# State products on 64-row halves of the array, attention on quarter-column tiles, first-pass stores on SyncE's queue

## The chip, the core and the metric

The kernel runs on one core of a Trainium2 chip. TensorE (PE) multiplies matrices into PSUM, VectorE (DVE), ScalarE (ACT) and GpSimd (POOL) work on tiles, SyncE (SP) issues most transfers; ACT and POOL issue some. Each engine and each queue works through its instructions in order. The metric is the device time of one execution in microseconds; lower is better.

## What is computed

Cross attention between a sequence and a small set of state vectors, then two gated feed-forward networks, all from float64-typed data on the host:

```python
scores = scale * x @ state.T            # B,H,S,Ns = 8,8,512,32; D = 64
a = softmax(scores);   xread = a @ state
a2 = softmax(scale * state @ x.T);  sread = a2 @ x
h = concatenate([xread, sread], axis=2)         # rows S + Ns, H*D = 512 wide
h = ((h @ w1) * (h @ w2)) @ w3 @ w_out          # first network, 4608 rows
out = (sigmoid(h @ w_gate) * (h @ w_val)) @ w_out2
```

## The kernel before

Most products are made of three passes over numbers split in two float32r parts (`split`: ACT writes the high part, DVE or POOL the rest), a few over plain float32.

**State products.** `xread` is never formed for the sequence rows. Since `xread @ w1 = a @ (state @ w1)`, the kernel first multiplies each head's state by that head's 64 rows of w1 and w2 and stores the result `sw` in DRAM (`sw_d`); a batch then needs `aT` (the softmaxed scores) times its own `sw`. The states lie in `bd` as block-diagonal 128x128 tiles: 128 contraction rows are two heads of 64, 128 columns are four blocks of 32 states, and the blocks that belong to the other head are zero. A step (`sw_step`, line 337) takes one 128x512 block of w1 or w2, which `sw_prep` has loaded as raw 64-bit words (`raw`), converted (`m`, `r`: two ACT operations, then three of DVE, the last on line 101) and split (`wh`: ACT, then POOL). It makes two products for two pairs of batches, three passes each, so six matmuls of 128 rows; ACT copies both to `swst`, and ACT's queue stores them. Sixteen steps are a pass. The first pass (`bp0` = 0) comes at the start, for half the batches; the second (`bp0` = 2) is spread over the batches at places 1 and 2 of the order, eight steps in each, between the groups `pab` and `py` of the first network.

**A batch.** `ffn1` runs over eight column blocks j: `sw_weights` loads a block of `sw` (`swf`, two transfers of 64 partitions) two blocks ahead and splits it (`swh`); twelve matmuls (`pab`) and the gate (`asb`, `u`) follow; then four groups of 24 matmuls (`py`) with the product of w3 and w_out. Between them stands the attention, by slots: the state's reads of this batch (`a2t`, `sread` line 240, `sreadt` line 258) and the transposes and `scores` (line 177) of the next. The order on TensorE is the order of the code; on the other engines and on SP's queue the Tile scheduler sets it in this part of the program.

**Scores and reads.** `scores` makes four float32 matmuls, each with 128 contraction rows (two heads, against the block-diagonal `bd`), 64 columns, and one half of the PSUM partitions. A float32 matmul runs as two passes, so the trace shows eight. `sread` makes sixteen of 128 rows and 64 columns over 128 moving columns; half of each result (the other head) is not used. `sreadt` transposes twice and copies twice.

The rest, from about 620 us, is the second network with its own planner; the change doesn't touch it.

## Time and profile before

| | us |
|---|---|
| median of 3 runs (1411.93 to 1413.6) | 1411.97 |
| the profiled execution | 1415.93 |
| its span, first to last instruction | 1414.2 |
| TensorE busy | 1343.5 |
| VectorE busy | 924.7 |
| ScalarE busy | 750.2 |
| GpSimd busy | 278.3 |

The page gives shares over the whole span; the stages have different limits, so the stretches are read one by one. The first pass ends at about 72 us, batch 0 at 195, batches 1 and 2 at 257.5 and 321.5; the last of the eight ends at about 589, and the first network's remaining rows at 620. Waits are put down to what came last before the waiting instruction.

### The profile page before, as it was taken

The numbers are of one execution on the slowest core, as the hardware profiler recorded it, in microseconds if no ns is written. First come the engines' busy times: TensorE is split into PE (matmuls) and PEld (weight loads), VectorE is DVE, ScalarE is ACT, GpSimd is POOL, SyncE is SP. The second block draws the span as 40 slices with busy tenths as digits, with TensorE's granted clock in tenths as the row PEclk, the third lists the DMA queues.
The fourth block names the chain that finished last, engine by engine and source line by source line (L and its number), as shares of the span: only waits on it lengthen the run. The fifth ranks groups of instructions, "written<-read, shape, count | busy, mean of one in ns | idle before, by whom it ended". The sixth has DMA issues, their size and how long they took to land.

```text
span 1414.2 us, 18988 instructions
## 1 busy us (share of the span) xinstructions
PE 1343.5 (95%) x6560; PEld 1145.6 (81%) x6560; DVE 924.7 (65%) x1523; ACT 750.2 (53%) x1480; POOL 278.3 (20%) x255
## 2 busy tenths in 40 slices
PE   5669999999998999999999999999999999999997
PEld 3348877777876777898988998988988888988996
DVE  6789756645555566528677667778777677556543
ACT  6877656756445456436546546545545544433421
POOL 2352113324334234001121121021121110000000
PEclk9889999999999999999999999999999999999999
DMA  9867637754446354383343347655445694134132
GB/s 264 290 195 212 199 135 230 228 195 127 138 119 164 90 155 152 118 319 116 133 151 100 117 165 285 239 183 169 136 167 184 227 324 159 62 108 137 49 104 67
DMA packets 169128, 237.18 MB, mean 168 GB/s; under 512 B 46920, under 2 KB 111944, under 8 KB 166984
## 3 DMA queue, kind: packets, MB, share of 16 engines
q1 hardware_dynamic: 130536, 163.15, 36.6%
q10 hardware_dynamic: 37344, 63.39, 12.8%
q0 software_dynamic: 1152, 9.44, 1.9%
q8 instruction: 51, 0.84, 0.2%
q14 instruction: 45, 0.37, 0.1%
HBM read 150.99 MB, written 84.93 MB: 167 GB/s over the span
## 4 chain that ended last, share of the span: by engine, by line
PE 80%; DVE 6%; issue 5%; DMA 4%; POOL 2%; ACT 2%; ACTq 0%; SPq 0%; DVEq 0%; POOLq 0%
PE po L1019 19%; PE psA L922 18%; PE psB L922 9%; PE pab L112 8%; PE py L112 7%; PE psC L922 5%; PE pab L115 4%; PE py L115 4%; DMA yf<-yd 2%; PE pwp L112 2%; POOL wh L66 2%; PE pwp L115 1%; PE psr L245 1%; PE pxt L170 1%; DMA raw<-in_moe_w 1%
## 5 line engine op out<-in xcount | busy, mean ns | idle before, releaser
L922 PE MATMUL psA<-y,wt 128*128 128x448 f32 (+1 forms) x1440 | 304.6, 360 | 5.6 <-ACT u L61 2.8
L922 PEld LDWEIGHTS psA<-y,wt 128*128 128x128 f32 x1440 | 266.3, 188 | 25.8 <-ACT u L61 3.9
L1019 PE MATMUL po<-wo,p 128*128 128x512 f32 x1224 | 280.7, 389 | 0.4 <-DVE p L590 0.4
L1019 PEld LDWEIGHTS po<-wo,p 128*128 128x128 f32 x1224 | 229.5, 188 | 48.3 <-DVE p L590 1.0
L922 PE MATMUL psB<-y,wt 128*128 128x448 f32 (+1 forms) x720 | 161.1, 359 | 0.0
L66 POOL TENSOR_TENSOR o<-m,o 128x256 fp32r<-128x256 f32 x72 | 59.3, 823 | 503.3 <-ACT o L61 449.1
L112 PE MATMUL pab<-aT,swh 128*128 128x512 f32 x512 | 145.7, 407 | 12.2 <-ACT asb L61 4.7
L922 PEld LDWEIGHTS psB<-y,wt 128*128 128x128 f32 x720 | 133.5, 188 | 8.5
L112 PE MATMUL py<-u,wp 128*128 128x512 f32 (+1 forms) x576 | 132.2, 381 | 2.1 <-DVE u L66 1.7
L61 ACT ACTIVATE u<-psA 128x448 f32<-128x448 f32 (+1 forms) x120 | 63.9, 532 | 127.7 <-PE psA L922 103.0
L112 PEld LDWEIGHTS py<-u,wp 128*128 128x128 f32 x576 | 104.0, 189 | 28.5 <-issue 5.7
L66 POOL TENSOR_TENSOR swh<-swf,swh 128x512 fp32r<-128x512 f32 x64 | 90.8, 1424 | 167.9 <-ACT swh L61 155.0
L112 PEld LDWEIGHTS pab<-aT,swh 128*128 128x128 f32 x512 | 95.3, 193 | 35.0 <-ACT asb L61 6.4
L61 ACT ACTIVATE p<-sg 128x448 fp32r<-128x448 f32 (+1 forms) x120 | 67.9, 566 | 86.6 <-DVE sg L958 79.0
L434 DVE TENSOR_TENSOR asb<-asb,pab 128x512 f32<-128x512 f32 (+1 forms) x72 | 47.0, 654 | 98.8 <-PE pab L115 90.3
L101 DVE CUSTOM_DVE_ANT_0 m<-m,r 128x1024 uint16<-128x1024 uint16 (+1 forms) x116 | 80.1, 692 | 11.1 <-ACT r L90 1.3
L66 DVE TENSOR_TENSOR u<-asb,u 128x512 fp32r<-128x512 f32 (+1 forms) x72 | 65.9, 916 | 30.7 <-ACT u L61 30.1
L1034 DVE TENSOR_TENSOR ob<-po,ob 128x512 f32<-128x512 f32 x68 | 46.8, 688 | 58.7 <-PE po L1019 55.4
L115 PE MATMUL pab<-aT,swh 128*128 128x512 f32 x256 | 81.7, 401 | 2.0 <-POOL swh L66 2.0
L922 PE MATMUL psC<-y,wt 128*128 128x448 f32 (+1 forms) x360 | 80.9, 360 | 1.1 <-DVE s L955 1.1
L61 ACT ACTIVATE y<-yf 128x448 fp32r<-128x448 f32 (+1 forms) x120 | 63.1, 558 | 32.4 <-DMA yf<-yd 32.4
L98 DVE SCALAR_TENSOR_TENSOR m<-raw,m 128x512 uint32<-128x512 uint32 (+1 forms) x116 | 78.2, 676 | 3.2
(118 smaller groups left out, 2028.3 us busy)
## 6 DMA issues: line engine op xcount, KB each, us to landing
raw<-in_moe_w SPq DMA_DIRECT2D x48, 512.0 KB, 5.6
wt<-wd SPq DMA_DIRECT2D x12, 1792.0 KB, 7.6
part<-ob SPq DMA_DIRECT2D x68, 256.0 KB, 2.8
ob<-part SPq DMA_DIRECT2D x68, 256.0 KB, 3.9
yf<-yd SPq DMA_DIRECT2D x37, 448.0 KB, 4.0
swd<-swst ACTq DMA_DIRECT2D x32, 512.0 KB, 4.1
swf<-swd SPq DMA_DIRECT2D x128, 128.0 KB, 3.7
wd<-o ACTq DMA_DIRECT2D x56, 256.0 KB, 2.3
```

Source lines behind the costliest of these rows:

```text
L61: return nc.scalar.activation(out=o, in_=i, func=AF.Copy)
L66: (sub or nc.vector).tensor_tensor(out=lo, in0=src, in1=hi.bitcast(F32), op=ALU.subtract)
L98: nc.vector.scalar_tensor_tensor(out=mu, in0=hi, scalar=0x80000000, in1=mu, op0=ALU.bitwise_and, op1=ALU.bitwise_or)
L101: nc.vector.tensor_tensor(out=m.bitcast(I32), in0=m.bitcast(I32), in1=r, op=ALU.add)
L112: nc.tensor.matmul(o, w[i], xx[k], start=n == 0 and i + k == 0, stop=False)
L115: nc.tensor.matmul(o, w[1 - late], xx[late], start=False, stop=n == len(pairs) - 1)
L170: nc.tensor.transpose(pt[:, c * P : (c + 1) * P], xn[b][:, g, c].rearrange("p a d -> p (a d)"), ident)
L245: nc.tensor.matmul(pt[64 * q : 64 * q + 64, k], t["a2"][:, k, c, 64 * q : 64 * q + 64], xn[b][:, 2 * k + q, c].rearrange("p a d -> p (a d) ...
L434: p2["dve"] = nc.vector.tensor_tensor(out=asb[:, :n], in0=asb[:, :n], in1=pab[1][:, :n], op=ALU.mult)
L922: nc.tensor.matmul(o, w[:, i, kb * P : (kb + 1) * P], xx[kb][h], start=start, stop=i == 1 and kb == 1, skip_group_check=True,)
L1019: nc.tensor.matmul(o, pt[j][i][:, s * P : (s + 1) * P], wot[j][:, h], start=j == js[0] and i + h == 0, stop=j == js[-1] and i == 1,)
L1034: nc.vector.tensor_tensor(out=ob, in0=o, in1=ob, op=ALU.add)
```

## The change

The states lie transposed but not block-diagonal, in `stT`: 64 rows are one head, the upper half of the partitions holds the even heads and the lower half the odd ones. A step still has six matmuls of 128 columns by 512, each with 64 contraction rows: the two heads' products go to two PSUM banks from the two halves of the array's rows. A step covers four consecutive batches, so the batches run in the order 0 to 7. `scores` has eight matmuls of 64 rows by 32 columns, `sread` 32 of 128 rows by 32 columns over 64 moving columns; `sreadt` has one transpose and one copy. Only half the states are turned at the start, the other half after the fifth step, and `z` is not cleared; six of its eight loads go out on ACT's queue. `swf` is one transfer of 128 partitions. In the first pass the stores of `swst` leave by SP's queue, in the second by ACT's.

```diff
-    sw_d = dram.tile([2, 2, 2, 2, P, B // 2, 512], F32, name="swd")
+    sw_d = dram.tile([2, 2, G, NS, 4, 2, 2, 512], F32, name="swd")
...
-                for k in range(2):
-                    pt = ps_at.tile([P, 512], F32, tag="at", name="psc")
-                    for q in range(2):
+                pts = [ps_at.tile([P, 512], F32, tag="at", name="psc") for _ in range(2)]
+                for g in range(G):
+                    for k in range(2):
                         nc.tensor.matmul(
-                            pt[64 * q : 64 * q + 64],
-                            bd[:, 2 * k + q, bp, b2 * 64 : b2 * 64 + 64],
-                            t["xT"][:, 2 * k + q],
+                            pts[k][NS * g : NS * g + NS],
+                            stT[64 * k : 64 * k + 64, g, b * NS : (b + 1) * NS],
+                            t["xT"][64 * k : 64 * k + 64, g],
...
-                        for q in range(2):
+                        for g in range(G):
                             nc.tensor.matmul(
-                                pt[64 * q : 64 * q + 64, k],
-                                t["a2"][:, k, c, 64 * q : 64 * q + 64],
-                                xn[b][:, 2 * k + q, c].rearrange("p a d -> p (a d)"),
+                                pt[NS * g : NS * g + NS, k],
+                                t["a2"][:, k, c, NS * g : NS * g + NS],
+                                xn[b][:, g, c, k],
...
-                for k in range(2):
-                    nc.tensor.transpose(
-                        pt[:, k].rearrange("p q h n -> p (q h n)"), t["sr"][:, k], ident
-                    )
+                nc.tensor.transpose(
+                    pt.rearrange("p g n -> p (g n)"), t["sr"].rearrange("p k d -> p (k d)"), ident
+                )
...
+        for b in range(B):
+            (nc.sync if b in (1, 3) else nc.scalar).dma_start(
...
-            products(*[(po[q], [([t[:, g, q] for t in bds], wh)]) for q in range(2)], late=1)
-            for q in range(2):
-                copy("act", st[:, q], po[q])
-            nc.scalar.dma_start(out=sw_d[hf, g % 2, g // 2, a, :, bp0 : bp0 + 2], in_=st)
+            for m, (x, w) in enumerate(((0, 0), (1, 0), (0, 1))):
+                for k in range(2):
+                    nc.tensor.matmul(
+                        po[k],
+                        sts[x][64 * k : 64 * k + 64, g],
+                        wh[w][64 * k : 64 * k + 64],
+                        start=m == 0,
+                        stop=m == 2,
+                    )
+            for k in range(2):
+                copy("act", st[:, k], po[k])
+            (nc.scalar if h4 else nc.sync).dma_start(
...
-        order = [q * (B // 2) + bp for bp in range(B // 2) for q in range(2)]
+        order = list(range(B))
...
-                for q in range(2):
-                    nc.sync.dma_start(
+                nc.sync.dma_start(
```

What moves in the order is shown at three places. TensorE in batch 1, at `sread` and the step behind it (`psr` are the reads, `psw` the products, `wh` the two parts of the weight block, `bds` or `sts` those of the states). Before:

```order
L115 MATMUL pab<-aT_1665,swh_1737 128x512 x2
L245 MATMUL psr<-xn,a2tr 64x128 x16
L112 MATMUL psw<-wh_1819,bds_1487 128x512
L112 MATMUL psw<-wh_1819,bds_1488 128x512
L112 MATMUL psw<-wh_1819,bds_1487 128x512
L112 MATMUL psw<-wh_1819,bds_1488 128x512
L115 MATMUL psw<-wh_1820,bds_1487 128x512 x2
L112 MATMUL pab<-aT_1665,swh_1770 128x512
```

Now:

```order
L115 MATMUL pab<-aT_1667,swh_1738 128x512 x2
L246 MATMUL psr<-xn,a2tr 32x64 x32
L344 MATMUL psw<-wh_1819,sts_1490 128x512 x2
L344 MATMUL psw<-wh_1819,sts_1491 128x512 x2
L344 MATMUL psw<-wh_1820,sts_1490 128x512 x2
L112 MATMUL pab<-aT_1667,swh_1770 128x512
```

The places are the same; the reads are twice as many and smaller, and the two matmuls of a row of the step now go to the two halves of the rows.

SP's queue from the start to the first loads of batch 0's `swf`. Before:

```order
L80 DMA raw<-in_moe_w 128x1024 x2
L290 DMA z<-in_state 32x16x64 x4
L80 DMA raw<-in_moe_w 128x1024
L155 DMA xn<-in_x 128x4x64 x8
L80 DMA raw<-in_moe_w 128x1024 x13
L465 DMA swf<-swd 64x4x128 x4
L80 DMA raw<-in_moe_w_out 128x1024
```

Now, from the eleventh weight block on:

```order
L80 DMA raw<-in_moe_w 128x1024 x2
L353 DMA swd<-swst 128x1024
L80 DMA raw<-in_moe_w 128x1024 x2
L353 DMA swd<-swst 128x1024 x2
L80 DMA raw<-in_moe_w 128x1024 x2
L353 DMA swd<-swst 128x1024 x5
L80 DMA raw<-in_moe_w_out 128x1024
L353 DMA swd<-swst 128x1024
L80 DMA raw<-in_moe_w_out 128x1024
L353 DMA swd<-swst 128x1024 x3
L475 DMA swf<-swd 128x4x128 x3
L80 DMA raw<-in_moe_w_out 128x1024 x2
```

The sixteen stores stand between the loads, and the first `swf` stands behind the last of them.

ScalarE in the second half of the first pass (`swst` are the copies of the products). Before:

```order
L61 ACTIVATE wh_423<-m 128x512
L345 DMA swd<-swst 128x1024
L89 ACTIVATE m<-raw 128x512
L90 ACTIVATE r<-raw 128x512
L61 ACTIVATE swst<-psw 128x512 x2
L89 ACTIVATE m<-raw 128x512
L61 ACTIVATE wh_448<-m 128x512
L345 DMA swd<-swst 128x1024
L90 ACTIVATE r<-raw 128x512
```

Now:

```order
L61 ACTIVATE wh_418<-m 128x512
L90 ACTIVATE r<-raw 128x512
L61 ACTIVATE swst<-psw 128x512 x2
L61 ACTIVATE wh_443<-m 128x512
L61 ACTIVATE swst<-psw 128x512 x2
L61 ACTIVATE wh_468<-m 128x512
L61 ACTIVATE swst<-psw 128x512 x2
L61 ACTIVATE wh_493<-m 128x512
L89 ACTIVATE m<-raw 128x512
L61 ACTIVATE swst<-psw 128x512 x2
```

`m` and `r` now run several steps ahead of the `wh` that rest on them, and the stores are gone from this queue.

## Rows read from the trace of the kernel before

**Rows 1.** The page's first part: busy us, share, instructions.
```profile
PE 1343.5 (95%) x6560; PEld 1145.6 (81%) x6560; DVE 924.7 (65%) x1523; ACT 750.2 (53%) x1480; POOL 278.3 (20%) x255
```

**Rows 2.** Stretches: length, busy by engine, granted clock, DMA share, GB/s.
```profile
core 0: us, PE busy (x) PEld busy (x) DVE busy (x) ACT busy (x) POOL busy (x), PEclk, DMA share, GB/s
5.50:35.60 30.10, 19.18 (x75) 12.86 (x75) 22.59 (x38) 22.71 (x44) 9.18 (x6) 0.89 0.97 280
35.60:72.30 36.70, 23.75 (x62) 13.31 (x62) 24.81 (x32) 29.84 (x55) 13.59 (x10) 0.81 0.83 282
75.00:115.00 40.00, 30.86 (x132) 22.55 (x132) 36.61 (x44) 28.52 (x53) 23.57 (x16) 0.83 0.73 196
...
195.00:257.50 62.50, 61.77 (x307) 49.60 (x306) 38.76 (x53) 42.95 (x78) 22.18 (x16) 1.00 0.61 188
...
321.50:545.00 223.50, 215.38 (x1082) 172.56 (x1081) 126.49 (x174) 120.11 (x215) 81.19 (x69) 0.98 0.44 130
...
620.00:1414.00 794.00, 777.81 (x3751) 695.45 (x3749) 534.07 (x959) 378.94 (x801) 90.70 (x104) 1.00 0.46 158
```

**Rows 3.** Timeline of TensorE in batch 1: start, length, instructions merged.
```profile
229.60 1.07 PE L112 MATMUL psw<-wh,bds 128*128 128x512 f32 x4
...
231.05 1.94 PE L186 MATMUL psc<-xT,bd 128*64 128x512 f32 x8
232.92 3.96 PE L112 MATMUL py<-u,wp 128*128 128x512 f32 x16
...
238.53 1.07 PE L112 MATMUL psw<-wh,bds 128*128 128x512 f32 x4
...
239.89 3.79 PE L112 MATMUL py<-u,wp 128*128 128x512 f32 x16
...
245.33 1.07 PE L112 MATMUL psw<-wh,bds 128*128 128x512 f32 x4
```

**Rows 4.** The same timeline, at the reads of the state.
```profile
207.73 1.07 PE L112 MATMUL pab<-aT,swh 128*128 128x512 f32 x4
...
209.18 1.97 PE L245 MATMUL psr<-xn,a2tr 128*64 128x128 f32 x32
211.08 1.19 PE L112 MATMUL psw<-wh,bds 128*128 128x512 f32 x4
...
212.58 1.07 PE L112 MATMUL pab<-aT,swh 128*128 128x512 f32 x4
```

**Rows 5.** Passes of `psc` and `psr`: ns, shortest, median, longest.
```profile
L186 PE MATMUL psc<-xT,bd x64: 592/592/643, 19.6 to 512.5; 128*64 128x512 f32 x64
...
L245 PE MATMUL psr<-xn,a2tr x256: 272/273/476, 107.4 to 548.6; 128*64 128x128 f32 x128
```

**Rows 6.** Timeline of TensorE: the transposes of `sreadt` in batch 1.
```profile
219.38 0.39 PE L261 MATMUL psrt<-ident,sr 128*128 128x128 f32 x2
```

**Rows 7.** ScalarE's waits from 35.6 to 72.3 us: total, times, longest.
```profile
ACT wh L61 <- DVE m L101: 5.6, 9, 0.7
```

**Rows 8.** SP's queue, first pass: start, length, transfers merged.
```profile
13.49 33.81 SPq L80 DMA_DIRECT2D raw<-in_moe_w  x13
51.00 3.80 SPq L465 DMA_DIRECT2D swf<-swd  x4
54.91 0.54 SPq L80 DMA_DIRECT2D raw<-in_moe_w_out  x1
```

**Rows 9.** Transfers from 0 to 75 us: count, KB, median us to landing.
```profile
raw<-in_moe_w_out SPq DMA_DIRECT2D x4, 512.0 KB, 5.1
...
swf<-swd SPq DMA_DIRECT2D x6, 128.0 KB, 6.2
```

**Rows 10.** Timeline of TensorE at the end of the first pass.
```profile
70.64 0.73 PE L115 MATMUL psw<-wh,bds 128*128 128x512 f32 x2 [0.18 <-POOL wh L66]
75.03 1.72 PE L112 MATMUL pab<-aT,swh 128*128 128x512 f32 x4 [3.66 <-ACT swh L61]
```

**Rows 11.** Timeline of TensorE in batch 5.
```profile
450.95 1.09 PE L170 MATMUL pxt<-ident,xn 128*128 128x128 f32 x4 [5.89 <-issue]
```

More of the change, by code (lines that the diff above doesn't have):

```diff
@@ L284, in tile_state_attention__then__gated_ffns, with state_turn @@
         tc.swap_default_side()
-        z = p1.tile([P, B // 2, G, 2, D], F32, name="z", bufs=1)
-        nc.vector.memset(z, 0.0)
-        for b2 in range(2):
-            for h2 in range(2):
-                p0 = b2 * 64 + h2 * 32
-                nc.sync.dma_start(
-                    out=z[p0 : p0 + NS, :, :, h2, :].rearrange("p b g d -> p (b g) d"),
-                    in_=state[b2 * (B // 2) : (b2 + 1) * (B // 2), h2::2].rearrange(
-                        "b g n d -> n (b g) d"
-                    ),
-                )
-        for g in range(G):
-            pt = ps_main.tile([P, 512], F32, tag="m", name="pt")
-            for bp in range(B // 2):
-                nc.tensor.transpose(
-                    pt[:, bp * P : (bp + 1) * P], z[:, bp, g].rearrange("p a d -> p (a d)"), ident
-                )
-            copy("act", bd[:, g].rearrange("p a b -> p (a b)"), pt)
-        def state_split(pool, bp0):
-            t = [pool.tile([P, G, 2, P], F32R, name=f"bds{i}", bufs=1) for i in range(2)]
-            for g in range(G):
-                split(t[0][:, g], t[1][:, g], bd[:, g, bp0 : bp0 + 2])
-            return t
+        z = p1.tile([P, 2, H, D], F32, name="z", bufs=1)
+        for b in range(B):
+            (nc.sync if b in (1, 3) else nc.scalar).dma_start(
+                out=z[b % 4 * NS : b % 4 * NS + NS, b // 4],
+                in_=state[b].rearrange("h n d -> n h d"),
+            )
+        def state_turn(h4):
+            pt = ps_main.tile([P, 512], F32, tag="m", name="pt")
+            for g in range(G):
+                nc.tensor.transpose(
+                    pt[:, g * P : (g + 1) * P],
+                    z[:, h4, 2 * g : 2 * g + 2].rearrange("p a d -> p (a d)"),
+                    ident,
+                )
+            copy("act", stT[:, :, h4 * P : (h4 + 1) * P], pt.rearrange("p (g m) -> p g m", g=G))
+        state_turn(0)
         def ahead(prep, depth, count):
@@ L354, in tile_state_attention__then__gated_ffns @@
         for i in range(2 * JF):
-            sw_step(i, 0, bds, wh(i), p1)
+            sw_step(i, 0, sts, wh(i), p1)
             if i == 0:
@@ L475, in prep @@
                 split(t[0], t[1], f, sub=nc.gpsimd)
-                return [[t[i][:, :, a] for i in range(2)] for a in range(2)]
+                return [[t[i][:, a] for i in range(2)] for a in range(2)]
             return ahead(prep, 2, JF)
```

61 lines of the change are left out of this document (34 added, 27 removed).

## The prediction

> **What bounds the kernel now.** I read the page's busy shares first: TensorE is busy nearly the whole span [rows 1], so the average says nothing about where a change can pay; the table by stage does [rows 2]. Four stretches matter. In the first pass of the state products (to about 72 us; the row is its second half) no engine is full: ScalarE is busy 29.84 of 36.70 us, VectorE 24.81, TensorE 23.75 at a mean granted clock of 0.81. In the start of batch 0 (75 to 115) VectorE is the bound, 36.61 of 40. From 115 us on TensorE is: 61.77 of 62.50 us in batch 1 (195 to 257.5), in which half of the second pass lies, and 215.38 of 223.50 in batches 3 to 6. The two gated-FFN passes after 620 us are TensorE's too, and the change touches nothing there. So TensorE time saved between 115 and 589 us counts in full as long as the others have room (in batch 1 ACT is busy 42.95 of 62.50 us, DVE 38.76), and in the first pass it counts for nothing: there the question is what the queues and ScalarE do.
>
> Then the timeline of TensorE inside batch 1 [rows 3, 4], which has the three kinds of matmul that change, each beside plain ones. A plain 128x512 one has a pitch of 0.227 us: six of `psw` from 238.53 to 239.89 are 1.36. The scores `psc` and the products `psr` already run on two 64-column halves of the array, and the rows show what that is worth: each pass of `psc` takes 592 ns and eight of them take 1.94 [rows 3, 5], so they run in four rounds of two, (1.94 - 0.59) / 3 = 0.45 us apart with the entry in it, 0.43 without. `psr`: 32 passes of 273 ns in 1.97 us, 16 rounds of two at 0.11. Two halves thus run at the same time without loss. And entering and leaving the halves costs: six `psw` last 1.45 before `psc` against 1.36, and the 24 `py` after it 5.61 (232.92 to 238.53) against 5.44 (239.89 to 245.33); with the 1.87 between, the excursion costs 0.09 + 1.87 + 0.17 = 2.13, of which 4 x 0.43 = 1.72 streams and **0.41 is the change of tiling**. For `psr` it is 0.09 + 1.90 + 0.14 = 2.13, with 1.74 of streaming and 0.39 of change. I use 0.40.
>
> **State products, second pass.** In batches 1 and 2 sixteen `sw_step`s of six matmuls stand between the `pab` and `py` groups, 1.36 us each. The change keeps six, but each has 64 contraction rows; the upper and the lower half of the array work for different heads and banks. Three rounds of two are 3 x 0.227 = 0.68, plus 0.40 for leaving and re-entering full tiling, since the neighbours stay full: 1.08, a gain of 0.28 x 16 = 4.5 us. No row has a matmul under 128 contraction rows. Bounds from the rows: halves overlap as the column halves do and the tiling change costs nothing where a step stands beside `psr` or `psc`, about -6; halves run one after the other, 1.36 + 0.40, +6.4. I take the overlap, because the column halves are the nearest row, and they overlap within one round. The Trainium skill (TensorEngine Tiling (Array Packing), Theoretical Speedup) gives up to 2x for a contraction of 64 or less, which would be that same 0.68; no run here shows it for rows.
>
> **Scores.** The four matmuls of 64 columns become eight of 64 rows by 32 columns, two passes each. If all eight tiles run together it is 2 rounds x 0.43 + 0.41 = 1.27 against 2.13: -0.86 in each of the seven batches whose scores lie in TensorE's stretch, **-6.0 us**. The first batch's lie in the first pass and count 0. The other bound is that only two column tiles stream at once, as now: 0.
>
> **Reads of the state (`sread`).** 16 matmuls of 64x128 become 32 of 32x64, so 64 passes instead of 32. With four tiles at once and half the columns it is 16 rounds x 0.055 + 0.40 = 1.27 against 2.13, -0.86 x 8 = -6.9. But per pass that is 14 ns, and the fastest pace in any row is 1.74 / 32 = 54 ns [rows 4]. If no faster pace is to be had, 64 x 0.054 + 0.40 = 3.86, +1.7 a batch, +14 in all. No row decides; the queue of instructions is filled during the plain matmuls before, which speaks for a burst. I take half the gain, **-3.5**.
>
> **`sreadt`.** One transpose instead of two, and one copy instead of two. Two of 270 ns take 0.39 [rows 6], so one less is 0.12 x 8 = **-0.9**. The copy is VectorE's and hidden.
>
> **First pass.** The order shows what moves. ScalarE loses the sixteen store issues; they cost it little (0.33 us on its queue, beside a running copy). More important, it now runs `m` and `r` of several steps ahead of `wh`, where before each `wh` waited for VectorE's last operation on the `r` issued just before: nine such waits are 5.6 us [rows 7], and ScalarE's whole idle time there is 36.70 - 29.84 = 6.9 [rows 2]. I count 7 us of it as removable at best. TensorE's half of the pass is hidden under ScalarE, so its halved matmuls bring nothing, as does the missing clear of `z` at the start, where the transfers are the limit. Against it stands SyncE. Its queue is in order, and each store waits there for ScalarE's copies; behind it are the loads of `raw`, and behind all sixteen the first loads of batch 0's `swf`. Before, `raw` went out in one run from 13.49 to 47.3 and the first `swf` at 51.00, over twenty us before use, with w_out from 54.91 on [rows 8]. The `raw` loads keep four and more steps of lead in the new order, so I cost that at nothing; what covers them is six buffers, and if the lead is gone each late one is a landing of about 5 us [rows 9]. But `swf` is now issued after the last copy: about 1.1 (copies) + 0.3 (store) + 0.6 (issue) + 6.2 (landing, rows 9) + 0.6 (`swh`) = 8.8 us after the last product, where the gap now is 75.03 - 71.37 = 3.66 [rows 10]: +5.1. Between them: **-2**, with ends -7 (idle gone, and VectorE fills the gap with w_out) and +5 (nothing gained, the gap longer).
>
> **Not in the sum.** At 445 us TensorE waits 5.89 us for a transpose [rows 11]: the copy that frees its bank stands on VectorE behind work that waits, over ScalarE, for a late `swf`. The order there is the same after the change, only with one `swf` transfer instead of two. If it goes, the time falls by up to 5.9; I leave it.
>
> **Sum.** -4.5 - 6.0 - 3.5 - 0.9 - 2 = -16.9. The profiled execution took 1415.93 us (its span 1414.2): 1399.0. It lay 3.96 above the median 1411.97, so against the median the forecast is **1395.1 us**.
>
> **Rivals.**
> (a) *The quarters give no more than the halves.* Scores and `sread` stay as they are, the rest holds: -4.5 - 0.9 - 2 = -7.4, 1404.6. For: no row has more than two column tiles streaming. Against: the two that do lose nothing.
> (b) *Slower: changes of tiling that aren't repaid.* If upper and lower rows take turns, each `sw_step` costs 0.40 more, +6.4; the scores, whose two row halves then take turns too, stay at four rounds (0), and `sread` gives nothing. With -0.9 and -2 it is +3.5: 1415.5. It decides at 0.40 of the 0.68 us: a step pays only if more than that overlaps. For: sixteen new excursions, each certain. Against: the overlap of the column halves.
> (c) *The pace of instructions.* 64 passes at 54 ns, +14 instead of -3.5: +0.6 in all, 1412.6. The Trainium skill (TensorE: Matmul & The Clock Gate, Back-to-back issue gap) names some 62 ns per matmul when the sequencer decodes in software; by it `sread` would take 64 x 0.062 + 0.40 = 4.4 us and the sum would be about +4.5, an estimate from that page; the 54 ns of this trace are already under it.
> (d) *SyncE's queue.* The first pass ends +5 and the late `swf` costs VectorE's stretch another 3: -6.9 in all, 1405.1. For: VectorE is nearly full from 75 to 115. Against: it has w_out to convert meanwhile.
>
> **How the numbers follow.** Forecast 0.58, (a) 0.14, (b) 0.10, (c) 0.08, (d) 0.10. A measurement tells about 0.2% (2.8 us) from no change. Forecast, (a) and (d) are faster, 0.82; (c) is within, 0.08; (b) slower, 0.10. The forecast's own range goes from -28 (first pass -7, products -6, `sread` -6.9, part of the wait at 445 us) to -8, and reaches over (a) and (d); leaving out (b), (c) and the far low end is about 0.2: 1384 to 1410.
>
> **What would show it.** In the profile after: `psw` matmuls starting in pairs, a step in batches 1 and 2 at 1.0 to 1.1 us from the `pab` before to the `pab` behind (1.7 for (b)); the sixteen passes of the scores in about 1.1 us from the first start to the last end (1.9 for (a)); `psr` under 1.5 us of 64 passes (3.5 for (c)); TensorE's stretch from batch 1 to batch 7 shorter by about 14; the first `pab` between 70 and 76 us, after a gap of 6 to 9 us behind the last `psw`. I am wrong if that stretch is not shorter, or if the first pass ends later than 80 us.

## Result and profile after

The changed kernel takes **1387.34 us** in the median (1385.52 to 1390.18), the kernel before 1411.95 beside it: a ratio of 0.9828, 95% interval 0.9807 to 0.9849, 24.6 us less. The forecast was 1395.1 with a range of 1384 to 1410. The profiled execution took 1387.57 us (span 1385.7), 28.4 less than the profiled one of before, which lay above its median.

First the page's busy line and the table of stretches, to be held against [rows 1, 2]; its columns are length, busy time by engine, granted clock of TensorE (1.00 is 2.4 GHz, 0.50 is 1.2), DMA share and GB/s.

```profile
PE 1310.1 (95%) x6864; PEld 1113.3 (80%) x6864; DVE 911.1 (66%) x1514; ACT 744.8 (54%) x1478; POOL 283.1 (20%) x255
...
35.60:72.30 36.70, 20.13 (x72) 10.46 (x72) 24.81 (x38) 29.20 (x55) 19.24 (x12) 0.55 0.75 268
75.00:115.00 40.00, 27.10 (x164) 20.06 (x164) 33.24 (x41) 28.08 (x51) 22.85 (x16) 0.87 0.79 225
195.09:253.53 58.44, 57.68 (x345) 43.09 (x346) 37.14 (x52) 41.63 (x78) 22.90 (x16) 1.00 0.62 199
312.66:511.11 198.45, 196.42 (x1189) 158.11 (x1188) 119.28 (x162) 110.94 (x200) 75.62 (x62) 1.00 0.45 142
```

The first line of the table is the second half of the first pass: ScalarE is about as busy as before (29.20 us against 29.84), VectorE is the same to the digit, GpSimd has gone up from 13.59 to 19.24, and TensorE's granted clock has fallen from 0.81 to 0.55. In the second line VectorE has 33.24 us of the 40 where it had 36.61. The two batch stretches are TensorE's, nearly without a gap, as before.

Where the time went is read from the start of each batch's first `pab` (first network) in the two timelines, us:

| stage | before | after | difference |
|---|---|---|---|
| start to the end of the first pass | 71.37 | 71.46 | +0.1 |
| gap before the first `pab` | 3.66 | 7.30 | +3.6 |
| batch 0 | 119.85 | 116.33 | -3.5 |
| batches 1, 2 | 62.69, 63.94 | 58.44, 59.13 | -4.25, -4.81 |
| batches 3, 4, 6 | 51.67, 51.67, 51.68 | 49.61, 49.62, 49.61 | -2.06 each |
| batch 5 | 58.43 | 49.61 | -8.8 |
| batch 7 | 51.10 | 47.86 | -3.2 |
| remaining rows | 34.55 | 34.55 | 0 |
| second network, to the last end | 793.54 | 792.16 | -1.4 |

So nothing came out of the first pass, 27.3 of the 28.4 us stand in batches 1 to 7, and a third in one batch. Two entries need care. Batch 0 took 119.79 us in a repeat of the changed kernel, so its -3.5 is not the change's. Of batch 7's -3.2 only 1.0 is the reads and their transpose. The rest is in its `py`: this one profile of before has waits of 0.42 and 1.68 us there and a granted clock of 0.75 from 564 to 570 us, the one of after a single wait of 1.45 at the full clock; in the run below of the kernel before with its stores moved the same batch took 48.39, so most of that is not the change's either.

The three kinds of matmul, in TensorE's timeline of batch 1 (start, length, instructions merged, tile shape, wait before):

```profile
204.91 0.61 PE L115 MATMUL pab<-aT,swh 128*128 128x512 f32 x2
205.46 0.97 PE L344 MATMUL psw<-wh,sts 64*128 64x512 f32 x6
206.35 1.20 PE L112 MATMUL pab<-aT,swh 128*128 128x512 f32 x4
207.39 0.62 PE L115 MATMUL pab<-aT,swh 128*128 128x512 f32 x2
...
209.30 1.10 PE L246 MATMUL psr<-xn,a2tr 128*32 128x64 f32 x64
210.33 0.96 PE L344 MATMUL psw<-wh,sts 64*128 64x512 f32 x6
...
228.38 1.09 PE L185 MATMUL psc<-xT,stT 64*32 64x512 f32 x16
229.40 3.93 PE L112 MATMUL py<-u,wp 128*128 128x512 f32 x16
```

From one start to the next, a step of six products is 0.89 us (205.46 to 206.35) where it was 1.36 [rows 3]; the 64 passes of the reads are 1.03 where 32 took 1.90 [rows 4]; the sixteen of the scores 1.02 where eight took 1.87. Summed over batch 1 by start-to-start times, `psw` falls from 11.22 to 7.17, `psr` from 1.90 to 1.03, `psc` from 1.87 to 1.02; the groups beside them (`pab`, `py`, `pxt`, `psrt`) rise by 1.52. Of that 0.14 lies in the batch's first four `pab`, which wait, and the rest stands beside the changes of tiling: a `pab` pair ahead of a step takes 0.55 (204.91 to 205.46) instead of 0.46, the four behind it 1.04 (206.35 to 207.39) instead of 0.91. The sum is -4.25, the stage's own difference.

The end of the first pass, to be held against [rows 10]:

```profile
69.31 2.15 PE L344 MATMUL psw<-wh,sts 64*128 64x512 f32 x6 [0.48 <-ACT wh L61]
78.76 1.65 PE L112 MATMUL pab<-aT,swh 128*128 128x512 f32 x3 [7.30 <-ACT swh L61]
```

At the lower clock (0.50 here) a step of half rows takes 2.15 us. The gap is within the 6 to 9 us forecast, since the first `swf` waits in SyncE's queue behind the last three stores, which wait for ScalarE's copies (row of its waits: total, times, longest):

```profile
68.06 4.91 SPq L353 DMA_DIRECT2D swd<-swst  x3
73.03 2.12 SPq L475 DMA_DIRECT2D swf<-swd  x3
...
SPq L353 <- ACT swst L61: 34.6, 16, 7.5
```

What became of ScalarE's idle time is the last reading. Its waits in the window of [rows 7], an early split (`wh`) by GpSimd, four later ones, the first of these alone, VectorE beside them, and TensorE behind them:

```profile
ACT swst L61 <- PE psw L344: 4.0, 1, 4.0
ACT wh L61 <- DVE m L101: 1.5, 3, 0.6
...
41.06 1.38 POOL L66 TENSOR_TENSOR wh<-m,wh 128x512 fp32r<-128x512 f32 x1 [0.38 <-ACT wh L61]
46.94 10.10 POOL L66 TENSOR_TENSOR wh<-m,wh 128x512 fp32r<-128x512 f32 x4 [4.51 <-issue]
...
46.94 6.26 POOL L66 TENSOR_TENSOR wh<-m,wh 128x512 fp32r<-128x512 f32 x1 [4.51 <-issue]
...
41.22 2.36 DVE L98 SCALAR_TENSOR_TENSOR m<-raw,m 128x512 uint32<-128x512 uint32 x2
...
46.52 1.28 DVE L98 SCALAR_TENSOR_TENSOR m<-raw,m 128x512 uint32<-128x512 uint32 x2
...
50.80 1.28 DVE L101 CUSTOM_DVE_ANT_0 m<-m,r 128x1024 uint16<-128x1024 uint16 x2
...
53.26 5.92 PE L344 MATMUL psw<-wh,sts 64*128 64x512 f32 x26 [5.17 <-POOL wh L66]
```

The waits for VectorE, 5.6 us before, are down to 1.5: ScalarE does run ahead, as the order promised. But then VectorE has its work in one unbroken run, from before 44 to 52 us, and in that run one split on GpSimd takes 6.26 us; the three behind it, from 53.20 on, take 1.28 each, once VectorE has stopped. TensorE waits 5.17 for it and ScalarE 4.0 for TensorE, about what was won at the waits for VectorE. The Trainium skill (SBUF — State Buffer, Who interferes with whom) says that an operation of VectorE with two inputs in SBUF and one of GpSimd that reads SBUF take turns at one port, as an exclusive lock; lines 98 and 101 have two inputs each, and the rows agree, with one thing more: GpSimd is held until the whole run ends, not for one operation. At 41 us it came first, and there VectorE's two operations of line 98 took 2.36 instead of 1.28. Spans on GpSimd are rough; TensorE's 5.17 us behind this one are not.

### The profile page after: what moved, and what is told of

It reads as the page before. It is cut to its first block, busy times and chain, and to the rows that moved or that the text cites. A ratio compares the mean times of both kernels' runs of the same rounds, so it can differ in the third digit from the quotient of the medians.

```text
span 1385.7 us, 19424 instructions
## 1 busy us (share of the span) xinstructions
PE 1310.1 (95%) x6864; PEld 1113.3 (80%) x6864; DVE 911.1 (66%) x1514; ACT 744.8 (54%) x1478; POOL 283.1 (20%) x255
## 4 chain that ended last, share of the span: by engine, by line
PE 80%; DMA 5%; DVE 5%; ACT 3%; issue 2%; SPq 1%; POOL 0%; ACTq 0%; DVEq 0%; POOLq 0%
PE psA L932 18%; PE po L1029 18%; PE psB L932 9%; PE py L112 8%; PE pab L112 8%; PE psC L932 5%; PE py L115 4%; PE pab L115 4%; DMA yf<-yd 2%; PE pwp L112 1%; DMA ob<-part 1%; PE psw L344 1%; PE pxt L169 1%; PE pwp L115 1%; DMA raw<-in_moe_w_out 1%
## 5 line engine op out<-in xcount | busy, mean ns | idle before, releaser
L112 PE MATMUL pab<-aT,swh 128*128 128x512 f32 x512 | 144.5, 404 | 16.2 <-ACT swh L61 7.3
L66 DVE TENSOR_TENSOR u<-asb,u 128x512 fp32r<-128x512 f32 (+1 forms) x72 | 63.1, 878 | 35.0 <-ACT u L61 34.6
L101 DVE CUSTOM_DVE_ANT_0 m<-m,r 128x1024 uint16<-128x1024 uint16 (+1 forms) x116 | 74.3, 644 | 13.5 <-ACT r L90 4.0
L89 ACT ACTIVATE m<-raw 128x512 f32<-128x512 f32 (+1 forms) x116 | 66.1, 571 | 29.3 <-POOL o L66 14.9
```

What stands on the lines that cost most here:

```text
L66: (sub or nc.vector).tensor_tensor(out=lo, in0=src, in1=hi.bitcast(F32), op=ALU.subtract)
L89: nc.scalar.activation(out=m, in_=hi.bitcast(F32), func=AF.Abs, scale=2.0**-112)
L101: nc.vector.tensor_tensor(out=m.bitcast(I32), in0=m.bitcast(I32), in1=r, op=ALU.add)
L112: nc.tensor.matmul(o, w[i], xx[k], start=n == 0 and i + k == 0, stop=False)
```

## Experiments

Each run had the kernel before beside it on its chip, so the difference to that is what compares between runs. In the changed kernel it is -24.6, and -20.4 in a repeat.

| kernel | median us | against before beside it | ratio, 95% |
|---|---|---|---|
| changed | 1387.34 | -24.6 | 0.9807 to 0.9849 |
| changed again | 1391.95 | -20.4 | 0.9829 to 0.9876 |
| stores on ScalarE's queue | 1397.58 | -16.2 | 0.9868 to 0.9905 |
| stores on GpSimd's queue | 1390.02 | -22.3 | 0.9823 to 0.9856 |
| before, stores on SyncE's queue | 1425.54 | +14.0 | 1.0062 to 1.0115 |
| all products on one row half | 1398.55 | -15.2 | 0.9877 to 0.9917 |
| `swf` in two transfers | 1395.80 | -17.9 | 0.9855 to 0.9902 |
| attention on 64-column tiles | 1408.95 | -4.8 | 0.9957 to 0.9981 |
| first pass on full rows | 1391.65 | -19.9 | 0.9823 to 0.9872 |
| early `swf` | 1389.41 | -22.1 | 0.9817 to 0.9865 |
| steps in pairs | 1390.65 | -20.9 | 0.9808 to 0.9868 |
| pairs, early `sreadt` | 1387.78 | -24.6 | 0.9805 to 0.9834 |
| the last version | 1386.49 | -26.0 | 0.9796 to 0.9841 |

**Do the row halves overlap?**

```diff
-                        sts[x][64 * k : 64 * k + 64, g],
-                        wh[w][64 * k : 64 * k + 64],
+                        sts[x][0:64, g],
+                        wh[w][0:64],
```

> In each step of the state products all six matmuls use the upper 64 rows of the array, so no two can overlap; the count, the shapes and the tiling stay. What is left out: the odd heads' products (the even heads' are computed twice). Theory 1 (the gain of a step is the overlap of the two row halves, and entering and leaving the tiling costs about 0.4 us all the same): a step in batches 1 and 2 takes 0.97 + 0.68 = about 1.65 us, 16 x 0.68 = 10.9 us more in all; about 1398, batches 1 and 2 some 5.4 us longer each, no other stage changed by over 1 us. Theory 2 (the halves overlap little, the gain of the batches came from the scores, the reads and the missing waits): a step stays under 1.2 us and the whole rises by less than 4 us.

```profile
206.72 1.66 PE L344 MATMUL psw<-wh,sts 64*128 64x512 f32 x6
208.31 1.19 PE L112 MATMUL pab<-aT,swh 128*128 128x512 f32 x4
```

A step takes 1.66 us instead of 0.97, three passes of 0.23 more, and batch 1 is 63.94 instead of 58.44: eight times 0.69. Batch 2 is 3.6 longer, less than the 5.4 expected (of the difference 0.8 is waiting that it had in the changed kernel and hasn't here); no other batch by 0.8. Theory 1 holds: the overlap of the halves is the step's whole gain, and without it the change of tiling makes a step dearer than before the change.

This run also shows the meeting of VectorE and GpSimd the other way round. Here the same four splits come at another point of VectorE's work, and VectorE is the one that is held:

```profile
48.86 6.55 POOL L66 TENSOR_TENSOR wh<-m,wh 128x512 fp32r<-128x512 f32 x4 [5.43 <-issue]
...
49.39 3.47 DVE L101 CUSTOM_DVE_ANT_0 m<-m,r 128x1024 uint16<-128x1024 uint16 x2
```

The four splits take 6.55 instead of 10.10, VectorE's two operations 3.47 instead of 1.28.

**Do eight and four tiles stream together?**

```diff
-                            pts[k][NS * g : NS * g + NS],
-                            stT[64 * k : 64 * k + 64, g, b * NS : (b + 1) * NS],
+                            pts[k][g // 2 * 64 : g // 2 * 64 + 64],
+                            stT[64 * k : 64 * k + 64, g, b // 2 * 64 : b // 2 * 64 + 64],
...
-                for k in range(2):
+                for k, h in ((k, h) for k in range(2) for h in range(2)):
                     for c in range(SC):
-                        for g in range(G):
+                        for q in range(2):
                             nc.tensor.matmul(
-                                pt[NS * g : NS * g + NS, k],
-                                t["a2"][:, k, c, NS * g : NS * g + NS],
-                                xn[b][:, g, c, k],
+                                pt[64 * q : 64 * q + 64, h, k],
+                                t["a2"][:, k, c, 64 * q : 64 * q + 64],
+                                xn[b][:, 2 * q + h, c, k],
...
```

> Scores and state reads on tiles of 64 columns, with the row halves and the 64 moving columns of the changed kernel and as many matmuls. What is left out: the right columns of the results (half of each tile belongs to another head, and a part is overwritten or not read). Theory 1 (the number of tiles that stream at once sets the time: eight for the scores, four for the reads): the sixteen passes of the scores take 1.09 + 0.43 x 2 = 1.9 us instead of 1.09, the 64 passes of psr 2.0 us instead of 1.10; batches 1 to 6 are 1.7 us longer each, the whole about 12 to 13 us slower. Theory 2 (the pace of issue or the change of tiling sets it): psc stays under 1.4 us and psr under 1.3, the whole within 4 us of the changed kernel.

```profile
212.81 2.09 PE L246 MATMUL psr<-xn,a2tr 128*64 128x64 f32 x64
...
233.22 1.96 PE L185 MATMUL psc<-xT,stT 64*64 64x512 f32 x16
```

With as many instructions of the same length, tiles twice as wide cost +0.99 and +0.87 us, what theory 1 said. Batches 3, 4 and 6 are 51.45, 51.47 and 51.48 long, 1.85 more each. The number of tiles that stream at once sets these times, not the pace of the instructions. That the whole is 16 to 20 us slower and not 13 is more than this explains; batch 5 took 53.71, two more than its neighbours, and batches 1 and 2 lost 2.7 and 2.2.

**What ended the wait at 445 us?**

```diff
-                nc.sync.dma_start(
-                    out=f.rearrange("p a k f -> p (a k) f"),
-                    in_=sw_d[b // 4, j // 4, :, :, b % 4, :, :, f0 : f0 + P].rearrange(
-                        "g n a k f -> (g n) (a k) f"
-                    ),
-                )
+                for q in range(2):
+                    nc.sync.dma_start(
+                        out=f[64 * q : 64 * q + 64].rearrange("p a k f -> p (a k) f"),
+                        in_=sw_d[
+                            b // 4, j // 4, 2 * q : 2 * q + 2, :, b % 4, :, :, f0 : f0 + P
+                        ].rearrange("g n a k f -> (g n) (a k) f"),
+                    )
```

> Each block of swf is loaded by two transfers of 64 partitions, as before the change; nothing else differs. Theory 1 (the wait of 5.89 us at 445 us before came from swf landing late, and one transfer instead of two is why it is gone): a wait of 4 to 6 us at a transpose of batch 5 comes back, batch 5 is 5 to 6 us longer than the 49.6 of the changed kernel, the whole 5 to 6 us slower. Theory 2 (it is gone because of the one copy of psrt and the shifted order, not because of the transfer): batch 5 stays within 1 us of 49.6, the whole within 2 us of the changed kernel.

In batch 5 of this kernel:

```profile
425.53 11.80 SPq L476 DMA_DIRECT2D swf<-swd  x8
...
434.07 0.63 ACT L61 ACTIVATE swh<-swf 128x512 fp32r<-128x512 f32 x1 [3.27 <-DMA swf<-swd]
435.26 1.36 DVE L66 TENSOR_TENSOR u<-asb,u 128x512 fp32r<-128x512 f32 x1 [3.21 <-ACT u L61]
440.30 0.28 DVE L264 COPY xst<-psrt 128x128 f32<-128x128 f32 x1
440.63 1.12 PE L169 MATMUL pxt<-ident,xn 128*128 128x128 f32 x4 [3.19 <-DVE xst L264]
...
440.00:447.00 7.00, 6.37 (x20) 5.15 (x21) 2.92 (x4) 3.96 (x7) 2.80 (x4) 0.53 1.01 247
```

and the same place of the changed kernel:

```profile
419.19 8.06 SPq L475 DMA_DIRECT2D swf<-swd  x4
...
431.61 0.66 PE L169 MATMUL pxt<-ident,xn 128*128 128x128 f32 x4 [0.51 <-DVE xst L264]
```

The wait is back and batch 5 is 55.08 us long, 5.5 more, with theory 1's chain in its rows: late `swf`, `swh` waits on ScalarE, `u` behind it, VectorE's copy behind `u`, TensorE behind the copy. The wait itself is 3.19 us, 2.7 more than in the changed kernel and short of the 4 to 6 expected; nearly all of the rest is the clock, which stands at 0.53 from 440 to 447 us where it is 1.00 in the changed kernel. Before the change, too, it was down behind the 5.89 us: 0.76 from 451 to 458. So of the 6.8 us that batch 5 gained beyond its neighbours (8.8 against 2.06), 5.5 are the one transfer instead of two. It was in the diff, and the prediction had traced the chain, but not asked whether the transfer in it would still be late.

**The stores of the first pass.** Three runs: back on ScalarE's queue; on GpSimd's; and on SyncE's in the kernel before.

```diff
-            (nc.scalar if h4 else nc.sync).dma_start(
+            nc.scalar.dma_start(
```

> The sixteen stores of the first pass go back to ScalarE's queue; all else as in the changed kernel. Theory 1 (SyncE's queue holds the first swf back, and that costs time): the first swf is issued before 55 us instead of at 73.03, the gap behind the last psw is about 3.7 us instead of 7.30, the first pab starts at about 75 instead of 78.76, and the whole is 3 to 4 us faster than the changed kernel, about 1384. Theory 2 (the gap is given back in batch 0, where VectorE is the bound and used the time for w_out): the gap closes too, but batch 1 still starts between 193.5 and 196 us (195.09 in the changed kernel) and the whole is within 1.5 us of the changed kernel.

```profile
41.34 1.06 ACT L61 ACTIVATE aT<-a2tr 128x1024 fp32r<-128x1024 f32 x1 [2.71 <-DVE a2tr L226]
...
74.72 2.15 PE L344 MATMUL psw<-wh,sts 64*128 64x512 f32 x6 [1.76 <-ACT wh L61]
80.77 1.65 PE L112 MATMUL pab<-aT,swh 128*128 128x512 f32 x3 [3.90 <-ACT swh L61]
```

Neither theory: the gap does close to 3.90, but the pass ends at 76.87 instead of 71.46, and the whole is slower by 4 to 8 us, not faster or the same. Without its run ahead ScalarE waits in line for the softmax of batch 0, 2.71 us with a `wh` behind it, and then for VectorE at every step.

```diff
-            (nc.scalar if h4 else nc.sync).dma_start(
+            (nc.scalar if h4 else nc.gpsimd).dma_start(
```

> The stores of the first pass leave by GpSimd's queue instead of SyncE's; nothing else differs. Theory 1 (what the move brought is that ScalarE's queue is rid of the stores; which other queue takes them matters little): the last psw of the first pass ends within 1.5 us of 71.5, the gap behind it is about 4 us, since the first swf doesn't stand behind the stores, and the whole is within 3 us of the changed kernel. Theory 2 (GpSimd is itself in the chain: it makes the low part of each wh, and a store that waits for ScalarE's copies holds the next one): waits of TensorE for the low part of wh grow by 1 us and more a step, the pass ends 3 us or more later, and the whole is over 4 us slower.

```profile
75.90 2.08 PE L112 MATMUL pab<-aT,swh 128*128 128x512 f32 x4 [2.28 <-ACT swh L61]
```

The pass ends at 73.62, 2.2 us later than with SyncE, the gap is 2.28, and the whole is within what the changed kernel itself varies by. Mostly theory 1: in this kernel what counts is that the stores are off ScalarE's queue. The gap is shorter by much more than it varies; the later end is not as sure, since with the first pass unchanged other runs ended it between 71.19 and 72.93.

```diff
-            nc.scalar.dma_start(out=sw_d[hf, g % 2, g // 2, a, :, bp0 : bp0 + 2], in_=st)
+            (nc.scalar if bp0 else nc.sync).dma_start(out=sw_d[hf, g % 2, g // 2, a, :, bp0 : bp0 + 2], in_=st)
```

> The kernel before, with the stores of its first pass on SyncE's queue and nothing else changed. Theory 1 (what the queue change brings is that ScalarE's work runs ahead, whatever the products): first pass ends 3 us or more before 71.37, the whole is 4 to 8 us faster than the kernel before, as the e1 run, 10 us slower without it, suggests. Theory 2 (it helps only with the slow steps of the half rows, or the prediction's own account holds): the first pass ends within 2 us of 71.37, the gap behind it grows from 3.66 to 7 us or more, and the whole is between 2 us faster and 5 us slower than the kernel before.

```profile
63.21 0.38 SPq L80 DMA_DIRECT2D raw<-in_moe_w  x1
...
ACT swst L61 <- issue: 7.5, 5, 2.2
ACT swst L61 <- PE psw L115: 6.6, 4, 2.6
```

The same move alone makes the kernel before 14 us slower, outside both theories: the pass ends at 78.99. Here the scheduler's order leaves the `raw` loads no lead: the last weight block goes out at 63.21 us, where it was 47.3 before [rows 8] and is 47.6 in the changed kernel. The prediction's sentence that the loads keep a lead is true of the changed kernel; the move itself is good or bad by the order that comes out of it. That the late loads are what costs the time here is argued, not shown: ScalarE's waits for `raw` come to 3.6 us in the pass and none falls behind 35.6, while its copies wait 6.6 for TensorE and 7.5 for something that the profile doesn't show.

**Does the low clock cost the first pass its gain?**

```diff
+            if h4 == 0:
+                t = [pool.tile([P, 2, G, P], F32R, name=f"sts{i}", bufs=1) for i in range(2)]
+                for i in t:
+                    nc.gpsimd.memset(i.bitcast(F32), 0.0)
+                for k in range(2):
+                    r = slice(64 * k, 64 * k + 64)
...
-                        sts[x][64 * k : 64 * k + 64, g],
-                        wh[w][64 * k : 64 * k + 64],
+                        sts[x][64 * k : 64 * k + 64, g] if h4 else sts[x][:, k, g],
+                        wh[w][64 * k : 64 * k + 64] if h4 else wh[w],
```

> The first pass alone goes back to products over all 128 rows, with zeros for the other head (two sets of states, cleared by GpSimd, split in halves); layout, order, stores, second pass and attention as in the changed kernel. Theory 1 (with half the rows TensorE's clock stays at the lower level in the first pass, 0.55 from 35.6 to 72.3 us against 0.81 before, a step takes 2.15 us there, and that is what ate the first pass's gain): the granted clock there is 0.75 or more, steps of 1.4 us appear, the last psw of the first pass ends before 69.5 us (71.46 in the changed kernel), and the whole is 2 to 4 us faster. Theory 2 (ScalarE and VectorE set the first pass, and TensorE's pace is hidden): the last psw ends within 1 us of 71.5, the whole within 1.5 us.

```profile
35.60:72.30 36.70, 23.63 (x70) 15.46 (x70) 25.22 (x37) 28.07 (x52) 19.66 (x11) 0.74 0.72 248
...
54.76 10.30 PE L353 MATMUL psw<-wh,sts 128*128 128x512 f32 x32 [4.63 <-POOL wh L66]
```

The clock comes back, nearly (0.74), and still the pass ends at 74.85, 3.4 us later, from the same start (first `psw` at 14.16, against 14.11). Behind the same long split TensorE now works through 32 products in 10.30 us, where the half rows took 5.92 for 26. Theory 1 falls: the half rows are worth something in the first pass even at 1.2 GHz. Theory 2 falls too, since TensorE's pace is not hidden there. The whole, -19.9, can't be told from the changed kernel.

**Is the longer gap a cost?**

```diff
+        nxt = sw_weights(order[0])
...
             if i == G:
                 state_turn(1)
+            if i == 11:
+                nxt(0)
```

> The first three loads of swf and their splits are called after the twelfth step of the first pass, so SyncE's queue has them before the last four stores; they need only the first eight steps' products. Theory 1 (the longer gap in front of batch 0 costs the whole): the gap behind the last psw falls from 7.30 to under 4 us, the first pab starts at 74.5 to 75.5 instead of 78.76, and the whole is 2 to 4 us faster. Theory 2 (batch 0 is VectorE's until 115 us and gives the gap back): the first pab starts earlier, but batch 1 within 1 us of 195.1, and the whole is within 1.5 us.

```profile
86.96 2.07 PE L112 MATMUL pab<-aT,swh 128*128 128x512 f32 x4 [4.46 <-ACT swh L61]
...
102.70 2.08 PE L112 MATMUL pab<-aT,swh 128*128 128x512 f32 x4 [5.41 <-ACT asb L61]
...
75.00:115.00 40.00, 25.84 (x150) 19.46 (x149) 35.62 (x43) 27.29 (x50) 19.31 (x13) 0.84 0.71 207
...
ACT wo L61 <- DVE m L101: 7.0, 6, 3.1
```

The gap is gone altogether, and the first `pab` starts at 72.30, 6.5 us earlier. Batch 1 starts at 196.63, no earlier than in the changed kernel (195.09, and 198.35 in its repeat). Theory 2, though its 1 us was too narrow: TensorE waits behind the gap's place instead of in it, for ScalarE, which itself waits 7.0 us for VectorE, and VectorE is busy 35.62 of the 40 us.

**The changed kernel again**, and why single traces of batch 0 say little:

> The changed kernel itself, beside the next two on the same chip. In the pairs run (e5) every instruction up to batch 1 stands in the same order as in the changed kernel, and still its batch 0 took 120.47 us instead of 116.33. Theory 1 (batch 0 varies by some us from execution to execution, and the profile of the changed kernel caught a short one): batch 0 here lies anywhere from 116 to 121 us, the median at 1386 to 1390. Theory 2 (it is the chip or another cause tied to the kernel): batch 0 repeats within 0.5 us of 116.3.

Batch 0 took 119.79 us here, 116.33 in the first profile, with the same order. Its stretch from 102 to 125 us, first profile ahead:

```profile
102.00:125.00 23.00, 18.93 (x138) 14.34 (x139) 22.54 (x31) 18.67 (x35) 11.13 (x8) 0.93 0.84 245
...
102.00:125.00 23.00, 17.82 (x121) 13.51 (x122) 22.54 (x30) 16.34 (x31) 9.95 (x7) 0.78 0.77 227
```

VectorE is full in both, 22.54 of 23.00; TensorE waits 3.27 instead of 1.57 us for it at the first `w3` transposes and its clock falls to 0.78. The median, 1391.95, lies above the range expected. Theory 1 holds, and differences of 2 or 3 us in this stage are not given to any edit below or above.

**Two ways to more.** Steps in pairs, to change the tiling half as often:

```diff
-                    slots[i + 3].append(
+                    slots[i // 2 * 2 + 3].append(
```

> The sixteen steps of the second pass stand two by two at every second place, eight excursions into the 64-row tiling instead of sixteen; the work is the same. Theory 1 (entering and leaving the tiling costs about 0.3 to 0.4 us each time, 0.97 - 0.68 by the changed kernel's step): two steps take about 1.65 us together instead of 1.94, batches 1 and 2 are 1.2 to 1.6 us shorter each, the whole 2.5 to 3 us faster. Theory 2 (the second step waits for PSUM: four banks are shared with pab, and ScalarE must copy two before the next pab): waits of 0.5 us and more appear behind the pairs, and the batches are no shorter or longer by up to 4 us each.

```profile
211.72 1.88 PE L344 MATMUL psw<-wh,sts 64*128 64x512 f32 x12
213.79 1.20 PE L112 MATMUL pab<-aT,swh 128*128 128x512 f32 x4 [0.19 <-ACT swst L61]
```

Two steps take 2.07 to the next `pab`, two single ones 2 x 0.89, and the neighbours of each excursion lose 0.09 + 0.13: 2.29 against 2.22, so nothing is saved where `pab` waits for ScalarE to empty a bank. That is theory 2, at a small size. By the batches it is mixed: batch 2 took 57.95 us, 1.2 less than in the changed kernel, as theory 1 said, of which 0.23 is less waiting; batch 1 took 63.29, with waits of 1.88 and 0.72 us at its start, the clock at the lower level for 6.9 us behind them, and a wait of 1.10 in `py`.

Pairs with `sreadt` one slot earlier:

```diff
-            after = {1: [lambda: a2t(0)], 2: [lambda: a2t(1)], 4: [sread], 6: [sreadt]}
+            after = {1: [lambda: a2t(0)], 2: [lambda: a2t(1)], 4: [sread], 5: [sreadt]}
...
```

> The steps of the second pass in pairs (as e5), and sreadt one slot earlier in every batch from the second on, so that VectorE's copy of psrt has a whole pab group more before the first pxt asks for a bank. Theory 1: two steps take 1.65 us instead of 1.94 (batch 2 took 57.95 us in the e5 run, 59.13 in the changed kernel), -1.2 us in each of batches 1 and 2, and the waits of 0.51 us before pxt in batches 3 to 6 go, -2.0; together about 4 us faster than the changed kernel beside it. Theory 2 (the waits come back at another place, or ScalarE's later copies hold pab): batches 3 to 6 stay at 49.6 us, and the whole is within 2 us of the changed kernel.

Batches 3 to 6 took 48.96, 48.93, 48.95 and 48.94, 0.66 less each: the wait of 0.51 before `pxt` is gone. Batch 1 took 62.03: TensorE waited 1.05 + 0.76 us at its start, its clock fell behind that (198.6 to 202.0), and there is a wait of 1.13 in `py`. The median is 4.2 us below the changed kernel's on the same chip, what theory 1 said, but the intervals touch (0.9805 to 0.9834 against 0.9829 to 0.9876), and in the profiles batches 2 to 6 gained 4.2 while batch 1 lost 3.6, so the sum fits partly by luck. In the last version the softmax of batch 1 also comes one group earlier, and the steps are single in batch 1:

```diff
-                    slots[i + 3].append(
+                    slots[i + 3 if t == 1 else i // 2 * 2 + 3].append(
...
+                if t == 0:
+                    slots[JF][4:4] = before.pop(6)
                 for i, fns in before.items():
-                    slots[i + 2 if t == 0 else i] += fns
+                    slots[i + 1 if t == 0 else i] += fns
```

> As e11 (sreadt one slot earlier), with three differences: the steps stand in pairs in batch 2 only, single in batch 1; in batch 0 the scores and the softmax of batch 1 come one py group earlier, its first transposes between two of the groups that multiply w3 and w_out. Theory 1 (the waits at the start of batch 1, 0.62 + 0.76 us in the changed kernel, 1.05 + 0.76 in e11, come from the softmax of batch 1 being late, and where they are long TensorE's clock falls behind them, 198.6 to 202.0 in e11): both waits are gone, the clock stays at its upper level from 125 us on, batch 1 takes at most 58.5 us, batch 2 57.9, batches 3 to 6 48.95 each; together 5 us faster than the changed kernel beside e11 (1391.95), about 1387 or a little less. Theory 2 (VectorE is behind in the whole of batch 0, so the softmax waits wherever it stands, and the wait moves to another place): batch 0 is longer by the same 1 to 2 us, and the whole is 1387.8 plus or minus 1.5, as e11.

The starts of batch 1, first in the run before this one, then in the last version:

```profile
197.29:203.00 5.71, 4.95 (x15) 3.74 (x16) 1.21 (x1) 1.54 (x3) 0.00 (x0) 0.70 0.12 46
...
195.41:201.00 5.59, 5.25 (x25) 4.06 (x24) 1.81 (x3) 3.16 (x6) 1.30 (x1) 1.00 0.14 50
```

Batch 1 is down to 57.91 at the full clock, but batch 2 now holds waits of 0.33 and 0.58 and a fall of the clock (266.9 to 270.3), and takes 61.69: the wait moved, as theory 2 had it, though not within batch 0. The median is the lowest of all, 1386.49; its interval overlaps that of the changed kernel, so it is not shown to be faster.

## Why the prediction came out as it did

The sign and the mechanism were right, the place was right but for the first pass, and the size was short by 3 to 8 us. Term by term:

- **Products, -4.5.** The working held: rounds of 0.23 us, and 0.43 instead of 0.40 for entering and leaving (0.09 before, 0.21 within the step, 0.13 behind, from the starts in the trace). That makes 0.25 a step, 2.0 for eight. Batch 1 gives 2.7 for its eight steps, so about -5.3 for both batches if batch 2 gives as much. The rest I put down to the two steps in eight that stand beside the reads and the scores and share their changes of tiling; no run tells it apart.
- **Scores, -6.0.** -0.85 a batch, as forecast.
- **`sread`, -3.5: mis-sized.** 1.03 us instead of 1.90, so -0.87 in each of batches 1 to 7 and -6.1 in all; in batch 0, where TensorE waits for others, the reads took as long as before. I had halved the gain for fear of a pace of 54 ns a pass, which was only the fastest that had been needed. Now 64 passes take 1.10 us, 17 ns each. The 62 ns per matmul that the Trainium skill (TensorE: Matmul & The Clock Gate, Back-to-back issue gap) gives for decoding in software would, by the prediction's estimate, have made that 4.4 us; the trace shows nothing of it.
- **`sreadt`, -0.9.** 0.11 a batch from batch 3 on, as forecast; in batches 1 and 2, where a step stands behind the transpose, it took 0.20 instead of 0.14.
- **The wait at 445 us, left out: the largest miss.** It went, worth 6.8 us of batch 5, more than the 5.9 that the prediction allowed, since the clock's fall behind it went as well. The order was the same, as I wrote, but one transfer of 128 partitions was out in a time in which two of 64 were not, and the run with two brought the wait back.
- **First pass, -2: the step that failed.** Its two halves were told apart: the removable 7 us of ScalarE against 5 us of gap. The gap came (7.30), the waits for VectorE went (5.6 to 1.5), and the pass ended where it had. The prediction asked only which engine ScalarE waits for, not what VectorE's unbroken run would do to GpSimd: behind one split of 6.26 us ScalarE waited 4.0, as much as it had won. That balance is read from the rows; no run takes this split alone away. The prediction's other sentence on the pass, that TensorE's half of it is hidden and the halved matmuls bring nothing, is wrong too: with full rows the pass ended 3.4 us later. And the gap doesn't count as such: batch 1 starts between 195.09 and 198.35 us with a gap of 7.30 or 7.37, of 2.28 (197.13) or of none (196.63). A pass that itself ends 5 to 8 us later does count: batch 1 then started at 201.97 (stores on ScalarE's queue) and, in the kernel before with its stores moved, at 206.15 instead of 194.88.

That the time fell inside the range is in part luck: the low end of the range had the full gain of the reads and part of the wait at 445 us, which came, but also 7 us of the first pass, which didn't. Of the signs named ahead, the lengths of the scores and the reads came true, and the step's 0.89 to 0.97 us lies just under the 1.0 to 1.1; the first `pab` started at 78.76 us and not between 70 and 76, and batches 1 to 7 were shorter by 27.3 us instead of about 14.

Of the rivals, (a), quarters no better than halves, and (c), the pace, are refuted by the reads and the scores and by the run on wider tiles; (b), row halves in turns, by the run on one half; (d), SyncE's queue, had its gap but no cost that a run could show.

The waits at the start of a batch, the clock's falls behind them and the second network (790.65 to 793.34 us in runs that don't touch it) are what remains between the sum and the medians. Why the kernel on wider tiles lost 5 us more than its matmuls, and why batch 0 varies, stay open.

## What to carry over

Where a matmul used half of the rows or a quarter of the columns, tiles that streamed together gave the whole factor here, less about 0.4 us for each excursion from full tiling: count the rounds and the excursions, and don't charge the passes for a pace that no row shows. When a trace holds a long wait whose chain you can follow, ask of every link whether the change touches it, above all the number and the width of its transfers, and count the clock that falls behind the wait with it. Taking work off an engine's queue frees what stands behind it, and that work then meets others: look at who shares a port, a bank or a queue with it, and at the order that the scheduler makes of it, before you count the idle time as won.

## What the hardware showed that was not expected

- **Half rows and the clock.** In the stretch from 35.6 to 72.3 us TensorE was busy 23.75 us with products of 128 rows at a granted clock of 0.81 [rows 2], 23.63 at 0.74 in the run with full rows, and 21.67 at 0.78 in the kernel before with its stores moved; with products of 64 rows it was at 0.55 with 20.13 us busy, and on one row half at 0.50, that is 1.2 GHz throughout, though busy 31.59 of 36.70 us. In batch 1 the steps of half rows stand between products of full rows, and there the clock was 1.00.
- **The clock behind short waits.** At the start of batch 1 waits of 1.05 + 0.76, 1.50 + 0.76 and 1.88 + 0.72 us were followed by 3.4 to 6.9 us at the lower clock; waits of 0.54 + 0.76, 0.62 + 0.76 and 0.86 + 0.76 were not. In batch 2 of the last version the shorter waits of 0.22, 0.33 and 0.58 between half-row products were followed by 3.4 us at the lower clock, so the length of the waits alone doesn't tell the two apart.
- **Tiles.** Eight tiles of 64x32 and four of 128x32 ran without loss to each other: sixteen passes of 589 ns in 1.09 us, 64 of 219 ns in 1.10.
- **Transfers by partitions.** In the 26 us around the wait in batch 5 one `swf` transfer of 128 partitions and 256 KB landed in 5.0 us in the median; transfers of half the size over 64 partitions took 6.1 there (7.0 in the kernel before), and there are two for each of the others. Over the whole of batch 5 the small ones took 4.6 us (4.2 in the kernel before) and the large ones 5.1, so a small one isn't slower as such; the slow stretch is the one in which eight went out in one row (425.53).
